# Batches 6 and 7 of an attention + ELU MLP kernel: their second layers as one product by seven half-size products, with attention ahead of the MLP

## The chip, the cores and the metric

The kernel runs on one core of a Trainium2 chip. The metric is the time of one execution on the device, in microseconds (us); lower is better. TensorE is called PE here (its weight loads PEld), VectorE DVE, ScalarE ACT, GpSimd POOL; SP issues the DMAs. Each engine works through its own instructions in the order in which the program issues them, and waits where an operand or a room is not ready.

## The reference

```python
def reference(q, k, v, g_q, g_k, w_in, w_out):   # q, k, v: 8 x 12 x 448 x 64
    q_n, k_n = rmsnorm(q, g_q), rmsnorm(k, g_k)  # over the last axis, eps 1e-6
    attn = softmax(q_n @ k_n.T / sqrt(64)) @ v   # for each batch and head
    x = attn.transpose(0, 2, 1, 3).reshape(8 * 448, 768)
    h = x @ w_in                                 # 768 x 2048
    g = where(h > 0, h, exp(min(h, 0)) - 1)
    return g @ w_out                             # 2048 x 768
```

## The kernel before

All products of the MLP are made with f16 operands, each f32 operand split in a high and a low f16 half; of the four partial products three are kept (high x high, high x low, low x high). So a first layer of a batch (`whi`, `wli` against `x`) is 16 rows `f` of 128 hidden units x 6 chunks x 3 = 288 matmuls of 448 columns, 18 to a row, and a second layer (`who`, `wlo` against `gts[f]`, the halves of g) is 6 rows `d` x 16 x 3 = 288. Products go to three PSUM banks in turn (`t_mo`); five more hold scores and the attention output.

Attention works in pairs of heads, six to a batch, a pair in seven tiles of 128 rows of scores: `s_burst` or `s_mm` (PE), `s_max` (DVE), `s_exp` (ACT), `s_z` (POOL), `s_rec` (DVE), `s_hi` (ACT), `s_lo` (DVE), a transposing DMA `s_tr`, then `attend` (PE) and `x_high`, `x_low`, which write the pair's chunk of x into one of nine rooms `xs`. Norms, halves and shifts of q, k and v are spread over POOL, DVE and ACT.

The order of all instructions is fixed by the program. Up to half step 264 (`H0`) it is a written list (`SCHED`); this part holds batches 0 and 1 of the MLP and is not touched. From there, two half steps make a tile of attention: in each half step `h` the tasks put at `h` are issued, and as many matmuls of the MLP as keep a steady rate (`RATE`, 6.86 in a half step). A product that ends at `h` puts its further steps at `h` plus the numbers in `SCHED` (`m1`, `m2`, `last1`, `last2`). After `LAST` (half step 700) seven matmuls are issued in each half step. `m1_out` is what follows a product of the first layer: `one` (ACT, exp), `two` (DVE), `three` (DVE, reads the product in PSUM and is its last reader), `four` (ACT, high half), `five` (DVE, low half).

The second layer of the last batch alone is already made by a scheme of seven products (Winograd's form of Strassen's): w_out is cut in 2 x 2 blocks (output rows `d` and `d + 3`, hidden rows `c` and `c + 8`), g in 2 x 2 blocks (hidden halves, and halves of 224 columns of the batch). Seven products of 24 matmuls of 224 columns for each of three `d` make it 504 matmuls of half width instead of 288 of full width. What the scheme needs of sums of weight blocks is made in twelve pieces beside attention (`piece_sums`, eight operations on DVE, two on ACT, two DMAs to DRAM, f32). At the end `t_steps` loads them back and splits them into halves (ACT and DVE, 24 operations each). The sums of the blocks of g are made in `m1_last` (ACT and DVE).

Of the kernel before, what the change touches and what calls it, by code (L numbers as in the profile page):

```python
# [33 lines left out]
def tile_attention_then_elu_mlp(ctx: ExitStack, tc: tile.TileContext, qk, v, v_scan, gg, w_in, w_out, out):  # L34
# [476 lines left out]
    def m_steps(b):  # L511
# [3 lines left out]
        sc = u = am = ui = ns = None  # L515
# [7 lines left out]
        def powers():  # L523
            nonlocal sc, u, am, ui, ns
# [6 lines left out]
            mscale[b] = sc, ui, u, ns, nui  # L531
# [8 lines left out]
        def inverse():  # L540
            ibits(ui, u, -1, ALU.mult, 254 * E, ALU.add)
            if b == 0:
                mul(mscale[b][4], ui, -1.0)
                mul(ns, ns, ui)

        def most_of():
# [5 lines left out]
            lambda: mul(u, am, vpow[b], 2.0 ** (-12 + UP)),  # L552
            inverse,
        ]
# [148 lines left out]

    def x_high(p):
        nc.scalar.activation(
            xs[p % NX][:, 0], av[:, :S], AF.Copy, scale=vscale[0] if by_pe(p * NJ) else 1.0
        )

    def x_low(p):
        x = xs[p % NX]  # L710
# [75 lines left out]
    HS, KF = S // 2, NF // 2  # L786
    scales = {}

    def joint_scales():

        t = pool.tile([128, 128], F32, tag="dgz", name="joint", bufs=2)
        pw, mx, rho1, rho2, uas_, aj, ui2 = (
# [3 lines left out]
        scales.update(rho1=rho1, rho2=rho2, uas=uas_, aj=aj, ui2=ui2)  # L796
# [7 lines left out]
    TS = ("t2", "t1", "t3", "t4")  # L804
    kept = [dram.tile([128, 4, 3, 256], F32, name=f"kept{d}") for d in range(3)]
    kept4 = [dram.tile([128, 4, 1, 256], F32, name=f"kept4{d}") for d in range(3)]
    tail = raws[:, 5 * S : 5 * S + 768].bitcast(F32)

    def piece_sums(d, r):

        A, Y, Z = (tail[:, a : a + 256] for a in range(0, 768, 256))
        W = None
        k = 4 * d + r
        rho = lambda i: scales[f"rho{i}"][:, k : k + 1]

        def full(o, row, kh):
            rows = slice(kh * KF, kh * KF + KF)
            h, l = (t[d + 3 * row][:, rows, 32 * r : 32 * r + 32] for t in (who, wlo))
            nc.vector.tensor_tensor(
                out=o.rearrange("p (f n) -> p f n", f=KF), in0=h, in1=l, op=ALU.add  # L820
            )

        def tt(o, x, y, op):
            nc.vector.tensor_tensor(out=o, in0=x, in1=y, op=op)

        def stt(o, x, i, y, op):
            nc.vector.scalar_tensor_tensor(
                out=o, in0=x, scalar=rho(i), in1=y, op0=ALU.mult, op1=op
            )

        def mul(o, i):
            nc.scalar.activation(o, o, AF.Copy, scale=rho(i))  # L832

        def fourth():
            nonlocal W
            W = pool.tile([128, 2 * S], F16, tag="p16", name="t4", bufs=3).bitcast(F32)[:, :256]
            full(W, 0, 1)
# [3 lines left out]
            lambda: mul(A, 1), lambda: tt(Z, Z, Y, ALU.subtract),  # L841
            lambda: stt(Y, Y, 2, A, ALU.subtract), lambda: mul(Z, 2), fourth,
            lambda: tt(A, Z, A, ALU.add),
            lambda: nc.sync.dma_start(
                out=kept[d][:, r], in_=tail.rearrange("p (q w) -> p q w", q=3)
            ),
            lambda: stt(W, W, 1, A, ALU.subtract),
            lambda: nc.sync.dma_start(out=kept4[d][:, r, 0], in_=W),
        ]

    stage = [t[:, a : a + 1024] for t, a in ((w32s, 0), (w32s, 1024), (wts, 0))]
    units = [
        t[:, a : a + 1024].rearrange("p (f r n) -> p f r n", f=KF, r=4)
        for t, n in (
            (raws.bitcast(F16), 6), (ptall.bitcast(F16), 6), (whis, 8), (wlis, 4),
        )
        for a in range(0, 1024 * n, 1024)
    ]
    part = [
# [37 lines left out]
    def t_step():  # L897
        if t_left:
            t_left.pop(0)()
# [774 lines left out]
UP = 13  # L1674
# [38 lines left out]
```

## Time and profile before

| | us |
|---|---|
| median of 3 runs | 1213.89 (1212.89 to 1215.51) |
| the profiled execution's own time | 1213.32 |
| its span, first to last instruction | 1211.2 |

The times are those of the program on the core. The rows further down come from the profiled execution; times in them count from the start of its span. `x24` is a number of instructions. "Busy" is the time in which at least one instruction of an engine was on record as running; a record that waits for something inside the chip counts as busy.

### The profile page before, as it was taken

The page shows a single profiled execution, that of the slowest core. Times are in us where ns is not written, and L with a number is a line of the kernel's source. Part 1 is how long each engine was busy: PE and PEld are TensorE (multiplying, and loading weights), DVE is VectorE, ACT ScalarE, POOL GpSimd, SP SyncE. Part 2 cuts the span into 40 slices and gives each one's busy share as a digit, 9 for nine tenths or more (in the row PEclk, how much of TensorE's full clock was granted, in tenths as well). Part 3 has the DMA queues.
Part 4 walks back from the last instruction along what each step waited for, and adds up shares of the span by engine and source line. Part 5 has one row for each costly group of instructions (what it writes and reads, how often), then busy time and mean ns, then how long its engine had stood idle before and what let it go on. Part 6 is the DMA issues. An engine that isn't in the chain of part 4 may idle for free. (4 is left out here: it accounts for less than half of the span.)

```text
span 1211.2 us, 22415 instructions
## 1 busy us (share of the span) xinstructions
PE 1168.8 (96%) x7396; PEld 632.7 (52%) x7396; DVE 1005.5 (83%) x2220; ACT 823.6 (68%) x1790; POOL 553.8 (46%) x799
## 2 busy tenths in 40 slices
PE   3789999999999999999999999999999999999998
PEld 2556555555455544445545545454554554555588
DVE  7999999888986699878997699878997799745962
ACT  6999999667866577656775577656776577644630
POOL 5887678654454343544444353544444454420000
PEclk9999999999999999999999999999999999999999
DMA  7876788868687866797669867797768976655200
GB/s 253 250 249 177 194 177 196 187 158 184 132 162 180 170 137 144 160 208 162 145 128 199 196 137 148 150 203 159 159 143 171 209 143 147 123 133 160 70 34 31
DMA packets 414531, 195.86 MB, mean 162 GB/s; under 512 B 369488, under 2 KB 394960, under 8 KB 414416
## 3 DMA queue, kind: packets, MB, share of 16 engines
q1 hardware_dynamic: 414416, 194.44, 70.8%
q8 instruction: 58, 0.95, 0.3%
q14 instruction: 57, 0.47, 0.1%
HBM read 74.65 MB, written 17.30 MB: 76 GB/s over the span
## 5 line engine op out<-in xcount | busy, mean ns | idle before, releaser
L625 POOL TENSOR_SCALAR st<-st 128x1 f32<-128x1 f32 x294 | 82.5, 281 | 400.5 <-ACT w32s L621 353.6
L605 DVE TENSOR_REDUCE st<-s 128x1 f32<-128x448 f32 x336 | 204.0, 615 | 52.8 <-PE s L598 42.2
L1134 PE MATMUL m<-gall,whos 128*128 128x448 f16 x896 | 242.7, 352 | 0.0
L621 ACT ACTIVATE w32s<-s,st 128x448 f32<-128x448 f32 x242 | 152.4, 630 | 104.6 <-DVE st L605 85.3
L1123 PE MATMUL m<-x,whis 128*128 128x448 f16 x816 | 221.0, 352 | 0.0
L671 DVE SCALAR_TENSOR_TENSOR raws<-w32s,st,raws 128x448 f16<-128x448 f32 x199 | 172.4, 867 | 30.8 <-ACT raws L665 30.4
L1134 PEld LDWEIGHTS <-whos 128*128 128x128 f16 x1344 | 130.7, 98 | 119.9 <-issue 1.8
L1123 PEld LDWEIGHTS <-whis 128*128 128x128 f16 x1344 | 130.3, 98 | 119.2 <-issue 2.7
L1134 PE MATMUL m<-gall,wlos 128*128 128x448 f16 x448 | 158.1, 353 | 0.0
L665 ACT ACTIVATE raws<-w32s,st 128x448 f16<-128x448 f32 x199 | 131.1, 663 | 22.1 <-DVE st L633 6.2
L1123 PE MATMUL m<-x,wlis 128*128 128x448 f16 x408 | 144.0, 353 | 0.0
L1134 PE MATMUL s<-gall,whos 128*128 128x448 f16 x448 | 121.3, 352 | 0.0
L598 PE MATMUL s<-qkt 128*64 128x448 f16 (+1 forms) x496 | 108.7, 363 | 12.8 <-DMA qkt<-t 4.9
L1123 PE MATMUL s<-x,whis 128*128 128x448 f16 x400 | 108.3, 352 | 0.2 <-DVE e L747 0.2
L1123 PEld LDWEIGHTS <-wlis 128*128 128x128 f16 x672 | 65.7, 98 | 69.7 <-issue 11.1
L1134 PEld LDWEIGHTS <-wlos 128*128 128x128 f16 x672 | 65.7, 98 | 69.3 <-issue 10.6
L407 POOL TENSOR_TENSOR nat<-nat,r 128x896 f32<-128x896 f32 (+1 forms) x48 | 87.3, 1819 | 31.7 <-DVE r L397 23.8
L698 PE MATMUL av<-ptall,vt 128*64 128x448 f16 x924 | 95.1, 353 | 0.0
L752 ACT ACTIVATE gall<-e,ui 128x448 f16<-128x448 f32 x96 | 63.8, 667 | 39.5 <-DVE e L747 39.4
L1134 PE MATMUL s<-gall,wlos 128*128 128x448 f16 x224 | 79.0, 353 | 0.0
L758 DVE SCALAR_TENSOR_TENSOR gall<-e,ui,gall 128x448 f16<-128x448 f32 x96 | 74.3, 775 | 1.3 <-ACT gall L752 1.3
L698 PEld LDWEIGHTS <-vt 128*64 128x64 f16 x924 | 52.0, 110 | 36.9 <-issue 3.2
(256 smaller groups left out, 2333.5 us busy)
## 6 DMA issues: line engine op xcount, KB each, us to landing
nat<-in_qk SPq DMA_DIRECT2D x48, 448.0 KB, 4.5
raws<-in_w_out SPq DMA_DIRECT2D x24, 512.0 KB, 4.2
qkt<-qkt SPq DMA_DIRECT2D x96, 112.0 KB, 4.1
out<-y SPq DMA_DIRECT2D x47, 224.0 KB, 2.4
vn<-in_v SPq DMA_DIRECT2D x38, 256.0 KB, 3.1
vscan<-in_v_scan SPq DMA_DIRECT2D x36, 224.0 KB, 3.3
whos<-in_w_in SPq DMA_DIRECT2D x10, 768.0 KB, 7.6
raws<-in_w_in SPq DMA_DIRECT2D x6, 768.0 KB, 7.2
```

The lines of the kernel that those rows point to most:

```text
L407: nc.gpsimd.tensor_tensor(out=n[:, a:], in0=n[:, a:], in1=r[:, a:], op=ALU.mult)
L598: nc.tensor.matmul(ps[r0 : r0 + n, :S], lhs, qq[:, 1, h * S : h * S + S], start=(t == 0), stop=(t == 2),)
L605: nc.vector.tensor_reduce(out=st[:, 0:1], in_=pss[T][:, :S], axis=AX.X, op=ALU.max, negate=True)
L621: nc.scalar.activation(e, ps, AF.Exp, bias=st[:, 0:1], accum_out=st[:, 1:2])
L625: (nc.vector if by_pe(T) else nc.gpsimd).tensor_scalar(out=st[:, 1:2], in0=st[:, 1:2], scalar1=1e-9, scalar2=2.0 ** (UP - 7) if by_pe(T) e ...
L665: nc.scalar.activation(p16[:, :S], e, AF.Copy, scale=stats[T][:, 2:3])
L671: nc.vector.scalar_tensor_tensor(out=p16[:, S:], in0=e, scalar=r, in1=p16[:, :S], op0=ALU.mult, op1=ALU.subtract)
L698: nc.tensor.matmul(av[64 * h : 64 * h + 64, :S], vs[:, h], ps[h], start=(k == 0), stop=(k == len(terms) - 1),)
L752: nc.scalar.activation(g[:, 0], e, AF.Copy, scale=1.0 if b == 0 else ui)
L758: nc.vector.scalar_tensor_tensor(out=g[:, 1], in0=e, scalar=ui, in1=g[:, 0], op0=ALU.mult, op1=ALU.subtract)
L1123: nc.tensor.matmul(ph[:, :S], w[:, c, :], x[:, r, :], start=(c == 0 and i == 0), stop=last)
L1134: nc.tensor.matmul(py[:, :S], w, g[:, r, :], start=(f == 0 and i == 0), stop=last)
```

## The change

The second layers of batches 6 and 7 become one product by seven. The two column halves are now the two batches of 448 columns. Batch 6 has its first layer as the other batches have it; then six products (`mid`) give the output rows `d` of batch 6 and with them `c11`, the first of the seven; then comes the first layer of batch 7, and then the other fifteen products (five for each of three `d`), all 448 columns wide: 6 x 24 + 15 x 24 = 504 matmuls.

- Both batches share one scale: `powers` takes the larger of the two `vpow`, `m_two` puts that earlier.
- `piece_sums` now writes high and low f16 halves to DRAM, four DMAs to a piece, by way of one room (`staging`, gained by putting both `k_up` into one room). Of its operations four (`full`) stay on DVE, twelve are on POOL, four copies on ACT. `SCHED["sums"]` puts a step of it every 1.18 half steps, before one every 2.7.
- The loads and splits of `t_steps` are replaced by 24 loads (`t_load`) straight into the rooms of `whis` and `wlis`, as the rows of the first layer of batch 7 are used up.
- `m1_last` is new: after `one`, `two` and `third` (as `three` before) it needs the difference of the two batches' g in place of batch 6's, and three more sums. `full` (POOL) adds batch 6's halves back to f32; the further steps are on DVE (`stt`, one `low_of`), ACT (`high`) and POOL (`full`, two sums, two `low_of`).
- Attention has three more rooms for x, and the rate of the MLP is set so that the first layer of batch 7 begins at half step 682 (`AHEAD`): from half step 264 on (3888 - 1179) / 418 = 6.48 matmuls in a half step.

```diff
-    k_up = [t.bitcast(F16)[:, :S] for t in rooms[NE : NE + 2]]
+    k_up = [rooms[NE].bitcast(F16)[:, a : a + S] for a in (0, S)]
     p_rooms = [t.bitcast(F16) for t in rooms[NE + 2 : NE + 2 + NP16]]
+    staging = rooms[NE + 1].bitcast(F16)[:, :512].rearrange("p (i n) -> p i n", i=2)
...
+            vp = vpow[b]
+            if b == B - 2:
+                vp = small("vp", bufs=1)
+                nc.vector.tensor_tensor(out=vp, in0=vpow[b], in1=vpow[b + 1], op=ALU.max)
...
-            mscale[b] = sc, ui, u, ns, nui
+            mscale[b] = (sc, *mscale[b - 1][1:]) if b == B - 1 else (sc, ui, u, ns, nui)
...
+    places, x_of = list(xs), {}
+
     def x_high(p):
+        if p == 3 * NPAIR:
+            for _ in range(3):
+                t = pool.tile([128, 2 * S], F16, tag="p16", name="xe", bufs=3)
+                places.append(t.rearrange("p (i s) -> p i s", i=2))
+        x_of[p] = places.pop(0)
...
+            o = o.rearrange("p (f r n) -> p f r n", f=2, r=4)
+            r = scales[f"rho{i}"][:, 4 * d : 4 * d + 4]
+            tt(o, o, r.unsqueeze(1).unsqueeze(3).broadcast_to([128, 2, 4, 32]), ALU.mult)
+
+        def split(o, q):
...
+            lambda: mul(A, 1), lambda: tt(Z, Z, Y, ALU.subtract), lambda: mul(Y, 2),
+            lambda: tt(Y, Y, A, ALU.subtract), lambda: mul(Z, 2),
+            *split(Y, "t1"),
+            lambda: tt(A, Z, A, ALU.add), lambda: full(Y, 0, 1),
+            *split(Z, "t3"),
+            lambda: mul(Y, 1), lambda: tt(Y, Y, A, ALU.subtract),
+            *split(A, "t2"), lambda: None, lambda: None,
+            *split(Y, "t4"),
...
+    def t_load(d, q):
+        for i in (0, 1):
+            nc.sync.dma_start(
+                out=part[d, q][i].rearrange("p c n -> p (c n)"), in_=kept[d][q][:, i]
+            )
...
+    def mid(d, kh, bank):
+        def first():
+            c11[d] = as_f32(places.pop(0))
+            nc.scalar.activation(c11[d], bank[:, :S], AF.Copy, scale=uas[d][0])
+
+        def second():
+            y = pool.tile([128, S], F32, tag="e", name="y", bufs=3)
+            more(y, bank, c11[d], uas[d][0])
+            return y
+
+        if kh == 0:
+            return "mid0", 0, [first]
+        y = []
+        return "mid1", 0, [lambda: y.append(second()), lambda: store(y[0], d, B - 2)]
...
+        c = f % KF
+        low = f < KF
+        g = gts[f]
+        e1, e2, r1, r2, r3, r4 = temps[c % 2]
+        e = e1 if low else e2
...
+        def third():
+            nc.vector.scalar_tensor_tensor(
+                out=e, in0=ph[:, :S], scalar=sc, in1=e, op0=ALU.mult, op1=ALU.max
+            )
+
+        def full(o):
+            nc.gpsimd.tensor_tensor(out=o, in0=g[:, 0], in1=g[:, 1], op=ALU.add)
+
+        def stt(o, x, s1, y, op):
+            nc.vector.scalar_tensor_tensor(out=o, in0=x, scalar=s1, in1=y, op0=ALU.mult, op1=op)
+
+        def high(o, x, s1=1.0):
+            nc.scalar.activation(o[:, 0], x, AF.Copy, scale=s1)
+
+        def low_of(eng, o, x):
+            eng.tensor_tensor(out=o[:, 1], in0=x, in1=o[:, 0], op=ALU.subtract)
+
+        if low:
+            return "last1", 0, [
+                one, two, third, lambda: full(r1),
+                lambda: stt(r2, e, scales["nui2"], r1, ALU.add),
+                lambda: high(g, r2), lambda: low_of(nc.gpsimd, g, r2),
+            ]
+        o1, o2, o3 = three
+        return "last2", 0, [
+            one, two, third, lambda: full(r4),
+            lambda: high(g, e, ui2),
+            lambda: nc.gpsimd.tensor_tensor(out=r3, in0=e1, in1=e2, op=ALU.add),
+            lambda: stt(g[:, 1], e, ui2, g[:, 0], ALU.subtract),
+            lambda: high(o1, r3, ui2), lambda: stt(r1, r3, ui2, r1, ALU.subtract),
+            lambda: high(o2, r1),
+            lambda: nc.gpsimd.tensor_tensor(out=r4, in0=r4, in1=r1, op=ALU.subtract),
+            lambda: stt(o1[:, 1], r3, ui2, o1[:, 0], ALU.subtract),
+            lambda: high(o3, r4), lambda: low_of(nc.vector, o2, r1),
+            lambda: low_of(nc.gpsimd, o3, r4),
+        ]
+
...
+    def mlp_two():
+        yield from first_layer(B - 2, range(NF), lambda k, f, ph: m1_out(B - 2, f, ph))
+        for d in range(3):
+            for kh in (0, 1):
+                bank = t_mo()
+                fs = range(kh * KF, kh * KF + KF)
+                for last in product(
+                    bank, lambda c: (who[d][:, fs[c]], wlo[d][:, fs[c]]), lambda c: gts[fs[c]]
+                ):
+                    yield mid(d, kh, bank) if last else None
+        t_left.extend((-(-4 * (i + 1) // 3) - 1, dq) for i, dq in enumerate(T_ORDER))
+        yield from first_layer(
+            B - 1, [k // 2 + k % 2 * KF for k in range(NF)], m1_last
+        )
+        for h in range(h_now[0] + 1, h_now[0] + 12):
             now, tasks[h] = tasks.get(h, []), []
             for fn, args in now:
...
+        for d, q in (
+            (0, "t3"), (0, "t4"), (1, "t3"), (1, "t4"), (0, "t1"), (0, "t2"), (0, "c22"),
+            (1, "t1"), (1, "t2"), (1, "c22"), (2, "t3"), (2, "t4"), (2, "t1"), (2, "t2"),
+            (2, "c22"),
+        ):
+            bank = made[d, q] = banks[n % 8]
+            n += 1
+            for _ in product(bank, lambda c: w_of(d, q, c), lambda c: b_of(q, c)):
+                yield None
+            ub, uj = uas[d][1:]
+            if q == "t2":
+                u2, u3, u4 = (as_f32(places.pop(0)) for _ in range(3)) if d < 2 else ys[0]
+                ys[d] = u2, u3, u4
+                more(u2, bank, c11[d], uj)
+                more(u4, made[d, "t1"], u2, uj)
+                more(u3, made[d, "t3"], u2, uj)
+                for k, row in (("t4", d), ("t1", d + 3)):
+                    y = pool.tile([128, S], F32, tag="e", name="y", bufs=3)
+                    more(y, made[d, k], u3, uj)
+                    store(y, row, B - 1)
+            if q == "c22":
+                y = pool.tile([128, S], F32, tag="e", name="y", bufs=3)
+                more(y, bank, ys[d][2], ub)
+                store(y, d + 3, B - 2)
...
-    START = HB + X_LAG
     LAST = 2 * NCHUNK + 28
+    pace = None
...
-        want = int((h + 1 - START) * RATE)
+        if pace is None:
+            base, pace = done, (FIRST_LAYER - done) / (AHEAD - h)
+        want = base + int((h + 1 - H0) * pace)
...
-    "scales": 671,
-    "sums": [272, 2.7],
-    "parts": [[676, 0.6], [690, 1.2], [716, 0.8]],
-    "last1": [[1, 2, 3, 4, 4, 5, 5, 6]],
-    "last2": [[1, 2, 3, 4, 4, 5, 5, 6]],
+    "scales": 640,
+    "m_two": [600, 602, 603, 604, 606],
+    "sums": [272, 1.18],
+    "mid0": [[1]],
+    "mid1": [[1, 2]],
+    "last1": [[1, 2, 3, 2, 4, 5, 6]],
+    "last2": [[1, 2, 3, 2, 4, 4, 5, 5, 6, 7, 7, 7, 8, 8, 9]],
...
-MLP_STEPS = 2 * 3 * (B - 1) * NF * NC_ + 3 * NF * NC_ + 3 * 7 * 12 + 1
+MLP_STEPS = 2 * 3 * (B - 2) * NF * NC_ + 2 * 3 * NF * NC_ + 3 * 7 * 24 + 1
+FIRST_LAYER, AHEAD = 2 * 3 * (B - 2) * NF * NC_ + 3 * NF * NC_ + 3 * 2 * 24, 682
 UP = 13
-RATE = 576 / (2 * PB)
-X_LAG = 8
```

## Rows read from the trace of the kernel before

**Rows 1.** Windows by stage: busy us (instructions) by engine, granted clock, DMA share, GB/s

```profile
60.00:90.00 30.00, 25.35 (x233) 17.18 (x233) 29.62 (x70) 27.46 (x59) 24.52 (x22) 1.00 0.77 248
133.40:200.10 66.70, 65.17 (x434) 34.45 (x430) 63.19 (x144) 62.62 (x131) 49.33 (x64) 1.00 0.83 186
969.00:1037.80 68.80, 68.80 (x406) 34.58 (x405) 65.65 (x138) 52.98 (x114) 32.47 (x46) 1.00 0.68 140
1105.10:1159.40 54.30, 54.30 (x289) 28.09 (x288) 47.75 (x100) 34.24 (x60) 0.00 (x0) 1.00 0.30 92
1159.50:1207.80 48.30, 48.30 (x506) 48.21 (x503) 18.25 (x38) 6.22 (x12) 0.00 (x0) 1.00 0.07 26
```

The columns of busy time are PE, PEld, DVE, ACT and POOL. The stages are a first layer in the written list (batch 0), the first layer of batch 6, the first layer of batch 7, and its second layer.

**Rows 2.** Chain that ended last, batch 7: start us, us, engine, product, line, matmuls

```profile
1105.23 3.40 PE m L1021 x18
...
1129.07 3.40 PE s L1021 x18
...
1187.31 4.60 PE m L1058 x48
1191.91 16.11 PE s L1058 x168
```

**Rows 3.** Timeline of DVE, the last `more`: start us, us

```profile
1208.05 0.45 DVE L1066 SCALAR_TENSOR_TENSOR y<-s,joint,uu 128x224 f32<-128x224 f32 x1 [1.85 <-PE s L1058]
```

**Rows 4.** Single source lines on DVE: ns min/median/max, first and last start, form

```profile
L819 DVE TENSOR_TENSOR raws<-whos,wlos x36: 405/415/985, 434.7 to 1030.8; 128x256 f32<-128x256 f16 x36
...
L671 DVE SCALAR_TENSOR_TENSOR raws<-w32s,st,raws x199: 658/683/1933, 323.1 to 1093.0; 128x448 f16<-128x448 f32 x199
...
L736 DVE TENSOR_SCALAR e<-e x96: 369/383/1221, 284.8 to 1039.7; 128x448 f32<-128x448 f32 x96
...
L747 DVE SCALAR_TENSOR_TENSOR e<-m,sc,e x64: 659/672/685, 285.4 to 1043.0; 128x448 f32<-128x448 f32 x64
...
L421 DVE TENSOR_TENSOR nat<-nat,gst x42: 599/616/1504, 9.8 to 1043.7; 128x448 f32<-128x448 f32 x42
```

These are `full` of the sums, `s_lo`, `two`, `three` and `q_gain`.

**Rows 5.** DMA issues: KB each, median us from issue to landing

```profile
out<-y SPq DMA_DIRECT2D x47, 224.0 KB, 2.4
...
wts<-kept SPq DMA_DIRECT2D x4, 512.0 KB, 5.2
...
kept<-t SPq DMA_DIRECT2D x12, 128.0 KB, 2.1
...
out<-y SPq DMA_DIRECT2D x2, 112.0 KB, 1.8
```

**Rows 6.** Single source lines on POOL, columns as in rows 4

```profile
L756 POOL TENSOR_TENSOR gall<-e,gall x16: 1033/1037/1602, 144.4 to 212.5; 128x448 f16<-128x448 f32 x16
...
L421 POOL TENSOR_TENSOR nat<-nat,gst x6: 1134/1482/1834, 21.7 to 105.1; 128x448 f32<-128x448 f32 x6
...
L472 POOL TENSOR_TENSOR vt<-vn,vt x38: 1154/1157/1542, 226.9 to 1085.4; 128x512 f16<-128x512 f32 x38
...
L407 POOL TENSOR_TENSOR nat<-nat,r x48: 1180/1690/2327, 8.6 to 1032.9; 128x896 f32<-128x896 f32 x47, 128x448 f32<-128x448 f32 x1
```

**Rows 7.** Timelines of DVE and POOL at two places

```profile
702.01 1.45 DVE L671 SCALAR_TENSOR_TENSOR raws<-w32s,st,raws 128x448 f16<-128x448 f32 x1
703.38 0.61 DVE L605 TENSOR_REDUCE st<-s 128x1 f32<-128x448 f32 x1
...
701.76 1.21 POOL L430 TENSOR_TENSOR t<-nat,t 128x448 f16<-128x448 f32 x1
...
709.89 0.41 DVE L819 TENSOR_TENSOR raws<-whos,wlos 128x256 f32<-128x256 f16 x1
...
710.82 1.50 DVE L671 SCALAR_TENSOR_TENSOR raws<-w32s,st,raws 128x448 f16<-128x448 f32 x1
...
709.83 2.01 POOL L407 TENSOR_TENSOR nat<-nat,r 128x896 f32<-128x896 f32 x1
```

**Rows 8.** Timeline of DVE, the third step behind the eighth product of batch 7

```profile
1134.35 0.68 DVE L937 SCALAR_TENSOR_TENSOR x<-s,sc,x 128x448 f32<-128x448 f32 x1
```

More of the change, by code (lines that the diff above doesn't have):

```diff
@@ L551, in m_steps @@
             scales,
-            lambda: mul(u, am, vpow[b], 2.0 ** (-12 + UP)),
+            lambda: mul(u, am, vp, 2.0 ** (-12 + UP)),
             inverse,
-        ]
+        ] if b < B - 1 else [powers, lambda: None, scales, lambda: None, lambda: None]
     def cuts(j):
@@ L826, in stt @@
[L826 to L829, printed above, removed]
-        def mul(o, i):
[L832 to L837, printed above, removed]
+            rows = slice(kh * KF + 2 * k, kh * KF + 2 * k + 2)
+            h, l = (t[d + 3 * row][:, rows].rearrange("p f n -> p (f n)") for t in (who, wlo))
@@ new lines, in m1_last, with one, two @@
+    def m1_last(k, f, ph):
+        sc, ui2 = (t[:, a : a + 1] for t, a in ((mscale[B - 1][0], f), (mscale[B - 1][1], 0)))
+        if not spots:
+            spaces()
+        c = f % KF
[3 more added lines that the diff above has]
+        e = e1 if low else e2
+        three = [as_f16(spots[i]) for i in range(3 * c, 3 * c + 3)]
+        sums.update(zip([("t1", c), ("t2", c), ("c22", c)], three))
+        def one():
+            nc.scalar.activation(e, ph[:, :S], AF.Exp, scale=sc)
+        def two():
+            nc.vector.tensor_scalar(
+                out=e, in0=e, scalar1=-1.0, scalar2=0.0, op0=ALU.add, op1=ALU.min
+            )
+        def third():
+            nc.vector.scalar_tensor_tensor(
+                out=e, in0=ph[:, :S], scalar=sc, in1=e, op0=ALU.mult, op1=ALU.max
[13 more added lines that the diff above has]
+                lambda: high(g, r2), lambda: low_of(nc.gpsimd, g, r2),
+            ]
+        o1, o2, o3 = three
[10 more added lines that the diff above has]
+            lambda: low_of(nc.gpsimd, o3, r4),
+        ]
@@ L1023, in mlp_last, with product @@
                     )
-                    yield m1_last(k, f, ph) if last else None
-        for h in range(h_now[0] + 1, h_now[0] + 8):
+                    if last and f == order[-1]:
+                        places.extend(x_of.pop(b * NPAIR + c) for c in range(NC_))
+                    yield result(k, f, ph) if last else None
+            while t_left and t_left[0][0] <= k:
+                t_load(*t_left.pop(0)[1])
+    def product(bank, w, x):
+        for c in range(KF):
+            for i, (a, r) in enumerate(((0, 0), (0, 1), (1, 0))):
+                nc.tensor.matmul(
+                    bank[:, :S], w(c)[a], x(c)[:, r],
+                    start=c == 0 and i == 0, stop=c == KF - 1 and i == 2,
+                )
+                yield c == KF - 1 and i == 2
@@ L1125, in mlp @@
                     )
+                    if last and f == NF - 1:
+                        places.extend(x_of.pop(b * NPAIR + k) for k in range(NC_))
                     yield m1_out(b, f, ph) if last else None
```

306 lines of the change are left out of this document (79 added, 227 removed).

## Prediction

> **What bounds the kernel now.** The page's first part counts PE as busy nearly throughout; a busy PE need not be a fast one, so next come the windows by stage: from 133 us on PE is busy for whole stages (68.80 of 68.80 us, 54.30 of 54.30, 48.30 of 48.30) at a granted clock of 1.00, which is the 2.4 GHz level [rows 1]. Third the chain that ended last: in the last batch seven products of 18 matmuls of 448 columns take 1129.07 - 1105.23 = 23.84 us, 189.2 ns each, and 48 of 224 columns take 1191.91 - 1187.31 = 4.60 us, 95.8 ns each [rows 2]. So the stage that changes is a queue of matmuls without gaps: a matmul less is time less, as long as nobody else makes PE wait. Who could? In a first layer beside attention DVE is busy 65.65 of 68.80 us and POOL 32.47; in the last first layer DVE 47.75 of 54.30 and POOL nothing [rows 1]. DVE has little to spare, POOL much.
>
> **The products.** Before, the second layer of batch 6 is 288 matmuls of 448 columns and that of batch 7 504 of 224: 288 x 0.1892 + 504 x 0.0958 = 54.5 + 48.3 = 102.8 us. After, both are 504 of 448 columns: 95.4 us. That is **-7.4 us** of PE time and all the change can win.
>
> **The end.** The last `more` is 448 instead of 224 columns wide: 0.67, as `three`, instead of 0.45 us [rows 3, 4]. The last store has 224 KB instead of 112: 2.4 instead of 1.8 us [rows 5]. With the longer last matmul **+0.9 us**.
>
> **Attention denser against the MLP, and the sums of weights.** The step rate falls from 6.86 to (3888 - 1179) / 418 = 6.48 matmuls per half step, so a first layer has 22.2 instead of 21 tiles beside it: DVE, ACT and POOL work of attention per PE time rises by 5 to 6%. Of the twelve pieces of sums DVE keeps four of eight operations, about 0.42 us each [rows 4], so it saves 12 x 4 x 0.42 = 20 us over the stage, which pays for that. ACT gets four copies for two products, about 1 us in a piece; it has room. POOL gets 12 x 12 = 144 operations of 256 columns. None is in the trace; at 448 columns one takes 1.04 us, at 512 1.16 [rows 6], 1.9 ns per column, so about 0.67 us, between 0.59 (in proportion to 448) and 1.04: 96 us of POOL, 17% of some 570 us. In a first layer POOL comes to 32.5 x 1.06 + 12 = 46 of 69 us. The SP queue gets 48 writes and 24 loads for 24 and 12; a load waits for the products of a few `f`, is of 256 KB (512 KB took 5.2 us [rows 5]) and is wanted some 40 us later. The staging room is refilled three steps, some 5 us, after its write is issued; a write of 128 KB took 2.1 us [rows 5], so I cost it at nothing; if SP is late, ACT waits there, and `s_exp` behind it. The nearest stage to all this is the window from 133 us: POOL 49.33 and DVE 63.19 of 66.7 us, PE 65.17 [rows 1], 1.5 us lost. Five such first layers (batches 2 to 6) bound it between 0 and 7.5 us; I take **+2.5**, a third, since DVE was fuller there. `s_rec` on DVE waits for `s_z` behind POOL's new work; that is in it.
>
> **The first layer of batch 7: the dear step.** PE makes two products (a pair, `f` = `c` and `c + 8`) in 36 x 0.1892 = 6.81 us. Per pair the new `m1_last` issues:
> on POOL six operations of 448 columns: two `low_of`, which have just the form of a row (1.04), two `full` (f16 to f32, not in the trace, 1.04 to 1.13) and two of f32 (1.13 [rows 6]), **6.4 us**. POOL alone is then 94% full.
> On DVE two `two` at 0.38, two `third` at 0.67, and five with both inputs in SBUF at 0.62 to 0.68 [rows 4]: 5.5 us. On ACT seven, at the 34.24 us for 60 of this stage before [rows 1] 4.0 us, which fits.
> Alone either engine fits. But the trace shows that such operations don't run at the same time. At 701.76 POOL begins an operation of the form that takes 1.04 alone, at 702.01 DVE one of 0.68; they take 1.21 and 1.45, and both are done at 703.46, 1.70 us for 1.72 us of work. At 709.83 a POOL operation of 1.69 alone meets two on DVE of 0.42 and 0.68: 2.49 us for 2.79 [rows 4, 6, 7]. `two` is hit as well (0.38 in the median, 1.22 at the most); `third`, which reads PSUM, is not (at most 0.69 in 96) [rows 4].
> So per pair: POOL 6.4, DVE's five and two `two` 4.1, less 0.5 because a DVE record overlaps the one before by 0.08 (703.38 against 703.46 [rows 7]): 10.0 us, and less the tenth that the second collision saved: **9.0 us for a pair** against PE's 6.81. In bounds: 6.81 if it all fits, 10.5 if nothing overlaps. I take 9.0, as the second collision has DVE and POOL work in about the mixture of this stage.
>
> The Trainium skill (GPSIMD Engine Reference, Specifications and Engine selection) speaks against this change twice: it says that GpSimd shares its SBUF interface with VectorE, which contend when DVE has two SBUF inputs or a two-port mode, and that two-input elementwise work takes about twice as long on GpSimd and belongs on VectorE. By the first the collisions above are the rule, and the trace agrees. By the second, six times 2 x 0.62 would be 7.4 us of POOL for a pair, an estimate, and the sum below would come to some 1227 us; the rows have 1.13 against 0.62 for one operation that both engines run [rows 4, 6].
>
> Why PE feels it: `third` frees the bank of its product, PE has three, so PE starts product k + 3 only when `third` of k is done, a slack of 6.81 us after product k ends. `third` stands in DVE's queue behind `g1`, `r1`, `o1`, `o2` of the pair before; `r2` and `r1` wait for POOL's `full` and `r3`, and POOL's `full` of two pairs on waits for DVE's `o2`: neither can run ahead. With the layer starting at 0, product 2 ends at 10.2; its `third` ends at about 13 (before, product 7 ended at 1129.07 + 3.40 = 1132.47 and its `third` at 1135.03 [rows 2, 8]). From there 9.0 a pair: `third` of product 12 at 13 + 45 = 58, so product 15 starts at 58 instead of 51.2, **6.8 us** late. Then (0, t3) wants `g` of row 7: `third` of product 14 ends at 67, then `r2` behind one POOL operation, ACT's copy, POOL's `low_of`, 3.6 us: 70.6. PE gets there at 58 + 3.4 + 21 x 0.19 = 65.4 and waits **5.2 us**. The three products after it, 13.7 us, cover the rest of the sums. Together **+12.0**; in general 6 x pair - 42, so 0 at 7.0 or less, 21 at 10.5. PE would be busy 55 of 62 us there; at 25.35 of 30 us the clock was 1.00 [rows 1], so no price for the clock.
>
> **Sum.** Against the profiled execution's own 1213.3 us: -7.4 + 0.9 + 2.5 + 12.0 = +8.0, **1221.3 us**. The median of the runs before is 1213.9, 0.6 higher, within their scatter.
>
> **Rivals.**
> A, faster: the collisions stay behind PE. A pair needs 7.0 us or less: POOL's `full` of f16 much shorter than 1.04, or POOL's queue filling the times in which DVE reads PSUM or waits for ACT. For it: PE hid a DVE at 95% and a POOL at 74% for 66 us. Against it: those busy times hold the collisions already, and here POOL's work alone is 94%. Time: -7.4 + 0.9 + 1 = -5.5, 1207.8. It decides from a pair of 7.6 us, where stall and saving cancel.
> B, the sums hurt too: POOL's 96 us collide with `s_lo` and `g1` in first layers that are 95% full on DVE, `s_rec` and so `s_exp` come late, PE waits for banks of scores. Price the upper bound and a little, 10 instead of 2.5: 1228.8. Against it: the stage from 133 us.
> C, no change: a pair of 7.3 to 8.0 us, stall 2 to 6, within 2.4 us of before.
>
> **How the numbers follow.** Forecast 0.48, A 0.26, B 0.14, C 0.12. 0.2% is 2.4 us, about what a measurement of this kernel can tell from nothing. Slower by more: forecast and B, 0.62; within: C, 0.12; faster: A, 0.26. The range leaves out the outer edges of A and B: 1207 to 1230; the forecast's own, with a pair of 8.3 to 9.8 us, is 1217 to 1227.
>
> **What would show it.** In the profile after: 504 matmuls of 448 columns at 189 ns in the last two second layers; in the first layer of batch 7 POOL over 90% busy, its operations and DVE's two-input ones well above 1.04 and 0.68; PE idle before products, released by DVE's `third`, some 7 us; one wait of some 5 us in (0, t3), released by POOL. Before that stage PE gaps of a few us in all. Wrong: POOL and DVE records overlapping without growing, the layer in 55 us, or gaps above 8 us before it.

## The result and the profile after

The changed kernel takes 1229.95 us (median of 4 runs, 1229.27 to 1233.49) against 1213.47 for the kernel before: a ratio of 1.0139 with a 95% interval of 1.0116 to 1.0162, so slower by 16 us where 8 were forecast. Its profiled execution took 1229.63 us, its span 1227.8.

The windows by stage of the changed kernel, columns as in [rows 1]: the whole stretch from batch 2's first layer to batch 7's, three pieces of it (a second layer and the first layer after it, and the last first layer beside attention), then the first layer of batch 7, and the fifteen products.

```profile
411.60:1088.20 676.60, 666.11 (x3904) 333.43 (x3902) 583.43 (x1180) 458.13 (x1028) 413.41 (x609) 1.00 0.78 160
482.80:554.10 71.30, 69.64 (x409) 34.92 (x408) 58.71 (x119) 45.22 (x106) 48.03 (x72) 1.00 0.92 185
554.10:627.30 73.20, 70.85 (x411) 34.87 (x410) 69.94 (x133) 53.61 (x122) 47.98 (x69) 1.00 0.70 146
985.00:1055.00 70.00, 70.00 (x411) 34.78 (x409) 63.22 (x136) 51.30 (x114) 34.77 (x56) 1.00 0.70 135
1088.20:1149.30 61.10, 56.40 (x288) 28.53 (x287) 52.95 (x59) 27.14 (x46) 46.53 (x36) 0.97 0.30 99
1149.50:1224.00 74.50, 69.88 (x361) 35.55 (x359) 24.67 (x32) 6.08 (x10) 13.51 (x11) 0.98 0.08 29
```

The same stretch and one first layer in it, of the kernel before:

```profile
412.40:1105.10 692.70, 690.54 (x4047) 346.31 (x4046) 576.08 (x1232) 458.94 (x1010) 298.11 (x469) 1.00 0.75 160
554.60:623.30 68.70, 68.70 (x405) 34.49 (x404) 65.60 (x138) 53.08 (x114) 32.25 (x46) 1.00 0.69 146
```

Read stage by stage. The long stretch, called the attention stage from here on, has 144 matmuls of 448 columns fewer, 27.2 us at 0.1892; before it would have been 692.7 - 27.2 = 665.5, now it is 676.6: **+11.1 us**. The last stage should be 54.3 us [rows 1] and 360 x 0.1892 = 68.1; it is 61.1 and 74.5: **+13.2 us**. The products save their 7.4 us. That is +16.9 for a span that grew by 16.6.

What PE waited for, the attention stage (releaser; us in total, times, longest us):

```profile
PE s L587 <- ACT w32s L626: 5.9, 9, 1.7
PE m L1103 <- DVE e L759: 2.4, 3, 1.2
PE av L703 <- issue: 1.2, 1, 1.2
```

and the last stage:

```profile
PE m L1015 <- DVE x L972: 3.7, 2, 2.1
PE s L1027 <- POOL gall L986: 2.5, 1, 2.5
PE s L1027 <- ACT gall L983: 2.1, 1, 2.1
PE s L1015 <- DVE rt L972: 1.0, 1, 1.0
```

In the first list PE waits for a bank of scores that an exponential (`s_exp`, L626) still has to read, and for a bank of the MLP that `three` (L759) has to free; `L1103` is a first layer. In the second stand the waits that were forecast: `third` (L972) frees the banks late, and the first product wants `g` of the last rows. Their sum is 9.3 of 13.2 us. In most of the rest PE worked at a lower granted clock. PE's timeline and the windows there:

```profile
1134.21 0.55 PE L1015 MATMUL m<-x,whis 128*128 128x448 f16 x2 [2.14 <-DVE x L972]
1134.58 0.55 PE L1015 MATMUL m<-x,wlis 128*128 128x448 f16 x1
```

```profile
1134.80:1137.80 3.00, 3.00 (x9) 1.21 (x8) 2.85 (x4) 1.77 (x4) 2.44 (x3) 0.50 0.01 4
1138.60:1142.00 3.40, 3.40 (x20) 1.76 (x19) 3.40 (x4) 1.20 (x2) 3.40 (x4) 1.00 0.12 30
1158.80:1161.80 3.00, 3.00 (x9) 1.21 (x8) 2.20 (x4) 1.34 (x2) 2.23 (x2) 0.50 0.03 5
```

Behind a wait of 2.1 us, and again behind 2.1 and 2.5, PE makes 9 matmuls in 3.0 us, 0.33 us each, at a granted clock of 0.50 (the 1.2 GHz level), and then 20 in 3.4 us at 1.00. Only the second fall cost time. The first stood, but for 0.2 us, in the place of a wait: it came in product 12, counted from 0, and product 14 began at 1142.70, 0.2 us after the end of the `third` that frees its bank (that of product 11, 1141.82 + 0.67), so at the full clock PE would have had to wait there. The timeline of `third` for products 2, 11 and 12, and PE's start of product 14:

```profile
1100.63 0.67 DVE L972 SCALAR_TENSOR_TENSOR rm<-m,sc,rm 128x448 f32<-128x448 f32 x1
...
1141.82 0.67 DVE L972 SCALAR_TENSOR_TENSOR rt<-m,sc,rt 128x448 f32<-128x448 f32 x1
...
1144.43 0.67 DVE L972 SCALAR_TENSOR_TENSOR x<-m,sc,x 128x448 f32<-128x448 f32 x1
```

```profile
1142.70 0.54 PE L1015 MATMUL m<-x,whis 128*128 128x448 f16 x2
```

The new instructions on POOL: three kinds of the sums (`mul`, f32 and low half), and three of the last first layer (`full`, `low_of`, `r3`):

```profile
L832 POOL TENSOR_TENSOR raws<-raws,joint x48: 607/614/1014, 434.1 to 1004.7; 128x256 f32<-128x256 f32 x48
L832 POOL TENSOR_TENSOR raws<-raws x48: 725/733/1130, 439.4 to 1006.9; 128x256 f32<-128x256 f32 x48
L832 POOL TENSOR_TENSOR wts<-raws,wts x48: 664/686/1182, 449.7 to 1018.1; 128x256 f16<-128x256 f32 x48
...
L977 POOL TENSOR_TENSOR rm<-gall x4: 1032/1416/1421, 1073.4 to 1147.4; 128x448 f32<-128x448 f16 x4
...
L986 POOL TENSOR_TENSOR gall<-rn,gall x4: 1037/1180/1409, 1096.4 to 1148.8; 128x448 f16<-128x448 f32 x4
...
L998 POOL TENSOR_TENSOR rn<-x,x x4: 1134/1244/1276, 1097.3 to 1151.3; 128x448 f32<-128x448 f32 x4
```

Alone (the shortest of each) they take about what was estimated (0.61 to 0.73 for 0.67, 1.04 and 1.13), and in the last first layer they stand stretched, as do DVE's in these rows (`two`, 0.38 alone [rows 4], and the low half of `g`):

```profile
L967 DVE TENSOR_SCALAR rt<-rt x4: 1217/1220/1319, 1105.1 to 1156.5; 128x448 f32<-128x448 f32 x4
...
L980 DVE SCALAR_TENSOR_TENSOR gall<-x,ui,gall x4: 979/1215/1226, 1097.8 to 1151.9; 128x448 f16<-128x448 f32 x4
```

### The profile page after: what moved, and what is told of

Read it like the earlier page. It is cut to its first block, busy times and chain, and to the rows that moved or that the text cites. A ratio compares the mean times of both kernels' runs of the same rounds, so it can differ in the third digit from the quotient of the medians.

```text
span 1227.8 us, 22061 instructions
## 1 busy us (share of the span) xinstructions
PE 1168.1 (95%) x7108; PEld 608.5 (50%) x7108; DVE 1024.3 (83%) x2122; ACT 815.0 (66%) x1792; POOL 729.0 (59%) x985
## 5 line engine op out<-in xcount | busy, mean ns | idle before, releaser
L626 ACT ACTIVATE w32s<-s,st 128x448 f32<-128x448 f32 x242 | 152.1, 629 | 121.9 <-DVE st L610 103.9
L610 DVE TENSOR_REDUCE st<-s 128x1 f32<-128x448 f32 x336 | 203.5, 613 | 30.9 <-PE s L603 22.2
L1116 PE MATMUL m<-gall,whos 128*128 128x448 f16 x768 | 209.7, 353 | 0.0
L1103 PEld LDWEIGHTS <-whis 128*128 128x128 f16 x1152 | 111.2, 98 | 110.8 <-issue 11.4
L1116 PEld LDWEIGHTS <-whos 128*128 128x128 f16 x1152 | 111.0, 98 | 107.9 <-issue 8.3
L1103 PE MATMUL m<-x,whis 128*128 128x448 f16 x578 | 157.6, 353 | 2.4 <-DVE e L759 2.4
L1116 PE MATMUL m<-gall,wlos 128*128 128x448 f16 x384 | 135.4, 353 | 0.0
L1116 PE MATMUL s<-gall,whos 128*128 128x448 f16 x384 | 105.3, 353 | 0.4 <-DVE gall L770 0.4
L1103 PE MATMUL m<-x,wlis 128*128 128x448 f16 x289 | 101.9, 353 | 0.0
L1103 PEld LDWEIGHTS <-wlis 128*128 128x128 f16 x576 | 56.3, 98 | 54.2 <-issue 3.3
L1103 PE MATMUL s<-x,whis 128*128 128x448 f16 x286 | 77.8, 352 | 0.3 <-DVE e L759 0.2
L1116 PE MATMUL s<-gall,wlos 128*128 128x448 f16 x192 | 67.7, 353 | 0.0
```

The costliest lines, as they stand in the source:

```text
L610: nc.vector.tensor_reduce(out=st[:, 0:1], in_=pss[T][:, :S], axis=AX.X, op=ALU.max, negate=True)
L626: nc.scalar.activation(e, ps, AF.Exp, bias=st[:, 0:1], accum_out=st[:, 1:2])
L1103: nc.tensor.matmul(ph[:, :S], w[:, c, :], x[:, r, :], start=(c == 0 and i == 0), stop=last)
L1116: nc.tensor.matmul(py[:, :S], w, g[:, r, :], start=(f == 0 and i == 0), stop=last)
```

## The experiments

All medians stand beside 1212.7 to 1213.8 us for the kernel before on the same chip. Theories: **collisions** (POOL's and DVE's instructions with two SBUF inputs run in turn, which fills the last first layer and stretches the others), against **density** (tiles of attention closer together make DVE the bound of the first layers, whatever POOL does) and **queue** (other work on POOL waits behind the sums). Stage times come from one execution of each version. For the versions in which the sums are taken apart it lies 1.1 to 1.8 us under the median of the runs, for the changed kernel 0.3, so differences between their stages are good to some 2 us.

### The sums, taken apart

`sums_idle` leaves out all arithmetic of the sums of weights (their rooms hold zeros); the DMAs stay.

```
...
     def full(o, row, kh):
...
-            nc.vector.tensor_tensor(out=o, in0=h, in1=l, op=ALU.add)
+            pass
     def tt(o, x, y, op):
+            return
             nc.gpsimd.tensor_tensor(out=o, in0=x, in1=y, op=op)
...
-                lambda: nc.scalar.activation(staging[:, 0], o, AF.Copy),
+                lambda: None,
...
```

> All arithmetic of the sums of weights is left out (DVE, ACT and POOL; the 48 writes and 24 loads stay and carry zeros), so the seven products of the last two batches are wrong. Theory sums (POOL's 144 operations collide with DVE beside attention): PE's gaps between the first layer of batch 2 and that of batch 7 fall from some 13 us to 4 or less, 1219 to 1222 us. Theory density (fewer MLP matmuls to a tile of attention make DVE the bound): the gaps stay, 1228 to 1231 us.

`sums_no_pool` leaves out POOL's twelve instructions of a piece only (the `return` alone).

> Only POOL's twelve operations of each piece of sums are left out (DVE's four, ACT's four copies and the DMAs stay; the sums are wrong). Theory sums by POOL's collisions: as without any arithmetic, 1219 to 1222 us, and s_lo on DVE falls from 903 ns back to about 870. If instead the staging room, ACT's copies or the DMAs were the cause: 1227 us or more.

`sums_memset` puts three memsets of a room that is not in use in the place of each.

```
...
-            nc.gpsimd.tensor_tensor(out=o, in0=x, in1=y, op=op)
+            for _ in range(3):
+                nc.gpsimd.memset(rooms[NE + 1][:, 256:448], 0.0)
```

> The changed kernel, with each of the 144 POOL instructions of the sums of weights replaced by three POOL memsets of a 128x192 f32 piece of a room that nothing uses then. POOL stays occupied at the same places, but reads no SBUF operands; the low halves of the sums' products are zeros and the combinations are not formed (the six DVE additions of a piece, the ACT copies and the DMAs stay). Without POOL's instructions the attention stage (batch 2's first layer to batch 7's) had taken 666.6 us, with them 676.6. Theory collisions (POOL's two-input instructions stretch DVE's two-input instructions, which bound the dense first layers): the stage goes back to 666 to 669, the run to about 1221. Theory queue (the per-tile scalar of the softmax waits on POOL behind the sums): the stage stays at 674 to 677, the run at about 1230.

Measured: 1217.54 us (1.0031, 1.0016 to 1.0046), 1221.19 (1.0071, 1.0056 to 1.0086) and 1227.52 (1.012, 1.0105 to 1.0135). The attention stage of the three, in this order:

```profile
411.90:1074.20 662.30, 662.09 (x3902) 332.28 (x3901) 535.83 (x1133) 443.58 (x980) 294.11 (x465) 1.00 0.79 164
```

```profile
411.60:1078.20 666.60, 663.57 (x3903) 332.70 (x3902) 558.53 (x1181) 457.15 (x1028) 293.54 (x465) 1.00 0.80 163
```

```profile
410.80:1083.50 672.70, 664.94 (x3903) 332.94 (x3902) 563.75 (x1181) 458.63 (x1028) 403.69 (x897) 1.00 0.79 161
```

Without the sums the denser attention costs nothing: 662.3, PE busy throughout. The DVE additions and ACT copies add 4.3 us (3.7 by the medians). Holding POOL for 110 us without reading operands adds 6.1 (6.3), in which DVE's busy time grows by 5.2. The real instructions, which read operands and hold POOL for 120 us, add the last 3.9 (676.6; by the medians 2.4), and with them DVE's busy time goes from 563.8 to 583.4 us: that is the stretch. So holding POOL costs at least as much as the stretch does.

In what the copies add there is a wait that the prediction had put at nothing: ACT stood 6.2 us in `sums_no_pool`, and 5.2 in the changed kernel, because the room `staging` had not yet been written out (`t<-wts` is the write; the line is of the changed kernel). No copy of ACT waited for POOL there.

```profile
ACT wts L841 <- DMA t<-wts: 5.2, 5, 2.1
```

`before_dense` gives the kernel before the changed kernel's pace (6.48 instead of 6.86 matmuls per half step, with the rooms for that) and leaves its sums and products as they were.

```
...
-        want = int((h + 1 - START) * RATE)
+        if pace is None:
+            base, pace = done, (FIRST_LAYER - done) / (AHEAD - h)
+        want = base + int((h + 1 - H0) * pace)
...
-RATE = 576 / (2 * PB)
...
+FIRST_LAYER, AHEAD = 3888, 682
```

> The kernel before with nothing of the change but the pace of 6.48 matmuls in a half step and three more rooms for x; the last 156 matmuls of batch 6 are made behind attention. Matmuls are as many as before. Theory density: some 9 us slower than before, 1222. Theory sums: within 3 us of before, 1211 to 1217.

Measured: 1220.06 us (1.0063, 1.0047 to 1.0079); its stage:

```profile
412.90:1110.90 698.00, 692.95 (x4048) 347.42 (x4046) 577.00 (x1232) 456.43 (x1010) 297.62 (x469) 1.00 0.76 158
```

698.0 - 27.2 = 670.8 against 665.5 at the old pace: density costs 5.3 us with before's sums, and the new form of the sums the other 5.8 of 11.1. Density costs nothing where DVE and POOL have no sums (`sums_idle`), so it is the two together that cost; the new form of the sums at the old pace was not run. The sums on POOL were meant to pay for the density; they cost as much again.

### The last first layer

`last_no_pool` leaves out POOL's six instructions of a pair (DVE and ACT read other operands, so the combinations are wrong).

```
-            nc.gpsimd.tensor_tensor(out=o, in0=g[:, 0], in1=g[:, 1], op=ALU.add)
+            pass
...
-            lambda: nc.gpsimd.tensor_tensor(out=r3, in0=e1, in1=e2, op=ALU.add),
...
+            lambda: None,
...
```

> POOL's six operations for each pair of products in the first layer of batch 7 are left out (DVE and ACT keep theirs, on other operands; results of the last two batches are wrong). By the collisions of this stage: the layer takes 54.5 us instead of 61.1, the wait in the first of the fifteen products and both falls of the clock go, 1216 to 1219 us. If DVE alone were too slow there: 1226 us or more.

`last_on_dve` computes everything: five of the six go to DVE (the expectation says six; the low half of `o3` stayed on POOL), and `two` goes to ACT as a Relu with signs turned.

```
...
-            nc.vector.tensor_scalar(
-                out=e, in0=e, scalar1=-1.0, scalar2=0.0, op0=ALU.add, op1=ALU.min
-            )
+            nc.scalar.activation(e, e, AF.Relu, scale=-1.0, bias=1.0)
...
-                out=e, in0=ph[:, :S], scalar=sc, in1=e, op0=ALU.mult, op1=ALU.max
+                out=e, in0=ph[:, :S], scalar=nsc, in1=e, op0=ALU.mult, op1=ALU.min
...
-            nc.gpsimd.tensor_tensor(out=o, in0=g[:, 0], in1=g[:, 1], op=ALU.add)
+            nc.vector.tensor_tensor(out=o, in0=g[:, 0], in1=g[:, 1], op=ALU.add)
...
```

> The changed kernel, with batch 7's first layer moved off POOL: the six POOL instructions of a pair of blocks go to DVE, and in exchange DVE's instruction on exp minus one goes to ACT as a Relu, with the sign carried by the constants; everything is computed. Theory collisions: a pair costs DVE 13 instructions at their unstretched 0.55 to 0.65 us, 7.2 to 7.6 us, against PE's 6.81 and against some 9 us now: the last first layer falls from 61.1 to 55 to 58 us, the wait in the first product shrinks to under 3 us, the granted clock keeps its upper level and the run is 1217 to 1221. Theory that DVE's amount of work alone is the limit: 13 instead of 8 instructions make a pair no shorter, the layer stays at 61 or above and the run at 1230 or above.

Measured: 1218.05 us (1.0045, 1.003 to 1.006) and 1218.08 (1.0046, 1.0029 to 1.0063). Layer and products of `last_on_dve`:

```profile
1088.80:1143.10 54.30, 54.30 (x289) 28.09 (x288) 48.45 (x83) 34.26 (x63) 12.92 (x6) 1.00 0.32 111
1143.30:1212.00 68.70, 68.13 (x361) 35.10 (x359) 20.24 (x33) 5.33 (x10) 3.35 (x2) 1.00 0.09 32
```

DVE issues 83 instructions in this layer instead of 59, having taken over five of POOL's six and given up only `two`, and is busy for less time, 48.45 instead of 52.95 us; the layer is at its 54.3. That shows the collisions, and 12.6 of the 13.2 us come back. `full` on DVE, its mean in ns behind the busy time (on POOL it took at least 1032, in the L977 line above):

```profile
L979 DVE TENSOR_TENSOR rm<-gall 128x448 f32<-128x448 f16 x4 | 2.5, 614 | 0.0
```

The granted clock stays at 1.00: without PE's waits it didn't fall.

### What POOL's sums delay

Three attempts to get at the queue, on the changed kernel: `s_z`, the 128x1 instruction between exponential and reciprocal, on DVE (`z_on_dve`) or on ACT (`z_on_act`), and the sums handed out in second layers only (`sums_in_second`).

```
-        (nc.vector if by_pe(T) else nc.gpsimd).tensor_scalar(
+        (nc.vector if by_pe(T) or T >= 132 else nc.gpsimd).tensor_scalar(
```

> The changed kernel, with the 128x1 instruction between the exponential and the reciprocal (s_z) on VectorE instead of POOL for all tiles from batch 2 on; everything is computed. Theory queue: reciprocals no longer wait behind POOL's sums, the stage falls from 676.6 to 667 to 670 us and the run to about 1222. Theory collisions: DVE, which is the bound of the first layers, gets some 200 more short instructions of 0.1 to 0.15 us while its stretch by POOL stays: the stage stays or grows to 680 to 690, the run is 1230 to 1240.

```
         nc.scalar.activation(e, ps, AF.Exp, bias=st[:, 0:1], accum_out=st[:, 1:2])
+        if not by_pe(T):
+            nc.scalar.activation(st[:, 1:2], st[:, 1:2], AF.Copy, scale=2.0**-7)
...
```

> The changed kernel, with the 128x1 instruction between exponential and reciprocal (s_z) on ScalarE, right behind the exponential, instead of on POOL; the added 1e-9 is left out, as the sum is at least 1. Everything else is computed. In the stage from batch 2's first layer to batch 7's, POOL's sums had cost 10.0 us, of which 6.1 remained when POOL was held as long by memsets. Theory queue (the reciprocal waits for s_z behind POOL's sums, and DVE's queue stands behind the reciprocal): those 6 go, the stage takes 669 to 672 us instead of 676.6 and the run 1222 to 1225 us. Theory that POOL's sums delay other work of POOL (V's parts, the normalising of Q and K) or that collisions on DVE are all of it: the stage stays at 675 to 678, the run at 1229 to 1231. ACT gets 294 instructions of about 0.2 us, some 40 us over the stage, of which it has 458 busy of 677.

```
...
-    "sums": [272, 1.18],
+    "sums": [0, [(306, 349), (395, 438), (484, 527), (573, 616), (661, 680)]],
```

> The changed kernel, with the steps of the sums of weights handed out only in the half steps in which the MLP is in second-layer products, where it puts no activation on DVE; everything is computed. Theory collisions with DVE as the bound of the first layers: the stage falls from 676.6 to 665 to 670 us (as without POOL's instructions or a little less), the run to 1219 to 1224. Theory that the density alone sets it, or that POOL's place doesn't matter: the stage stays at 674 to 677 and the run at 1228 to 1231. Loss if the sums are now packed too densely for POOL: above 1231.

Measured: 1241.58 us (1.0238, 1.0222 to 1.0255), 1253.06 (1.0319, 1.0299 to 1.034) and 1239.58 (1.0218, 1.0201 to 1.0235), all worse than the change. PE's two waits in the stage of `sums_in_second`, and a wait of ACT there:

```profile
PE av L703 <- DMA ptall<-raws: 9.4, 7, 4.2
PE s L587 <- ACT w32s L626: 8.4, 6, 2.1
```

```profile
ACT wts L841 <- DMA t<-wts: 46.4, 24, 3.9
```

The attention products wait for transposes of the probabilities (`ptall<-raws`), and for exponentials, that come late. But this run changed two things: packed into second layers, the sums stand almost twice as close together (312 steps in 191 half steps, before in 367), and ACT, which makes the exponentials and the high halves, stood 46.4 us for the room `staging` (5.2 in the changed kernel). So it doesn't show whether the tiles in second layers have room for POOL's hold.

With `s_z` on ACT, DVE's largest wait in the stage is the first line here; the second is the same wait in the changed kernel:

```profile
DVE raws L679 <- ACT raws L673: 44.3, 61, 2.6
```

```profile
DVE raws L676 <- ACT raws L670: 22.8, 39, 1.8
```

So neither engine takes 0.14 to 0.2 us more on each tile's way from the exponential to its low half without loss. That `s_z` itself waits behind the sums is little of it. Three waits for POOL in the stage, of DVE for `s_z` (in the changed kernel and in `sums_memset`) and of ACT for `ua`, the factor with which a second layer's output is scaled (changed kernel):

```profile
DVE st L638 <- POOL st L630: 1.2, 3, 0.8
```

```profile
DVE st L638 <- POOL st L630: 2.5, 4, 1.1
```

```profile
ACT y L791 <- POOL ua L783: 6.2, 5, 2.6
```

The wait for `ua` is 6.5 us in `sums_memset`, and there is none in the kernel before or in `sums_no_pool`. It is the largest that the sums add on POOL, and behind it stand ACT's exponentials; that PE's stops come from it is not shown.

`last_on_dve_z_on_act`, that edit and `last_on_dve` in one, took 1239.17 us where 1211 to 1214 or 1218 was expected. `sparser_sums`, the same with the sums 1.33 half steps apart, took 1237.6, where 1210 to 1212, 1 to 2 us less than the other, or no change was expected. Both missed their level by more than 20 us, and their intervals overlap. On the kernel before:

> The kernel before, with s_z on ScalarE alone. POOL had no sums there, s_rec waited 5.5 us for POOL in all, and in the stage PE was stopped for 0.7 us. Queue theory: there was hardly a queue, so 1212 to 1214 us, no change. If a shorter way from the exponential to the reciprocal is worth something in itself: under 1211.

1216.22 us (1.0027, 1.0017 to 1.0037): a loss there too.

### Giving DVE room

On top of `last_on_dve`, two ways to relieve DVE in first layers: an uneven pace (fewer tiles beside first layers, more beside second ones), or every `two` on ACT as in the diff above.

```
...
-        want = base + int((h + 1 - H0) * pace)
...
+        left = 1.0
+        while left > 0:
+            end = (int(reach + 1e-6) // 288 + 1) * 288
+            r = pace[int(reach + 1e-6) % 576 // 288]
+            dt = min(left, (end - reach) / r)
+            reach, left = reach + dt * r, left - dt - 1e-9
+        want = int(reach + 1e-6)
```

> As last_on_dve (1218 us; stage from batch 2's first layer to batch 7's 677.1 us), with the pace of the MLP uneven: 6.86 matmuls per half step in first layers, as before, and 6.11 in second layers, the same 6.48 on average and the same end of attention. Everything is computed. Theory (DVE is the bound of the dense first layers, where it is busy 67 to 70 of 70 to 73.5 us, and has 10 us of room in the second): first layers lose their stalls of 1.4 to 4.7 us each, the stage falls to 666 to 671 us and the run to 1207 to 1212. Rival (the amount of work on POOL and in the loop of DVE and ACT sets it, wherever the tiles stand; or second layers then stall as they did with the sums packed into them): the stage stays at 674 to 680, the run at 1215 to 1221.

> The same with 7.20 in first and some 5.85 in second layers. Theory: first layers now free of stalls, second layers at 1.11 times the density of the average; if these have room, as uneven_686 or 1 to 2 us better; if their transposes come late, as in sums_in_second, worse than uneven_686 by 3 or more. Rival: no change from last_on_dve.

> As last_on_dve, with the exp-minus-one instruction of every batch's first layer (two, 0.38 us on DVE) on ACT as a Relu (some 0.56 us), sign carried by the constants; even pace. DVE is relieved of 16 x 0.38 = 6 us in a first layer, ACT gets 9 on top of 53 of 73. Theory (DVE is the bound): the stage falls to 668 to 672 us, the run to 1209 to 1213. Rival (the loop through ACT is as full, as with s_z on ACT, where DVE waited 20 us more for ACT's high parts): the stage grows to 680 or more, the run to 1221 or more.

Measured: 1221.38 us (1.0063, 1.0047 to 1.0079), 1218.19 (1.0047, 1.0032 to 1.0063) and 1211.09 (0.998, 0.997 to 0.9989). With the uneven pace the stage took 678.2 and 677.0 us; its first layers from batch 3 on were faster (69.8, 68.7, 69.2 and 68.8 us at 6.86), and PE waited for late transposes instead:

```profile
PE av L703 <- DMA ptall<-raws: 4.5, 3, 2.1
PE s L587 <- ACT w32s L626: 3.2, 5, 1.4
```

So moving tiles moves the stall. Taking work from DVE removes it: in `two_on_act` the stage fell to 663.8 us, but an interruption in batch 1's first layer let batch 2 start at 419.0 instead of 411.6. (Both together, `uneven_two_on_act`, took 1216.81, between the two, where 1205 to 1211 was expected.) The last pair leaves batches 0 and 1 alone, on `last_on_dve` and on the kernel before:

```
...
         def two():
...
+            if b > 1:
+                nc.scalar.activation(e, e, AF.Relu, scale=-1.0, bias=1.0)
+                return
...
```

> As two_on_act (1211 us), but from batch 2 on only. Batch 1's first layer, which had a stall of 8.6 us in two_on_act, is as in the changed kernel. Theory (DVE is the bound of the dense first layers): the stage takes 663 to 666 us as in two_on_act, and the run 1202 to 1206 us, 0.6 to 0.9 per cent under before. Rival (the late start of batch 2 in two_on_act is what gave its stage room): the stage grows back to 668 to 672 and the run is 1208 to 1212.

> The kernel before with the same edit, from batch 2 on. Theory: in the kernel before DVE was full but not late (PE was stopped for 2.1 us between 412 and 1105 us), so at most 2 us can be won: 1211 to 1213 us. Rival (a gain of its own): 1208 or less. With a loss through ACT: above 1214.

Measured: **1206.52 us (0.9935, 0.9922 to 0.9948)**, 0.5 above the range expected, and 1209.39 (0.9961, 0.9948 to 0.9974). The stage of `two_from_batch_2`, a first layer in it, and its last two stages; then the stage of `before_two_on_act`:

```profile
412.30:1077.40 665.10, 663.07 (x3903) 332.34 (x3902) 554.55 (x1109) 492.67 (x1108) 407.48 (x607) 1.00 0.80 163
...
554.50:624.90 70.40, 70.09 (x410) 34.81 (x409) 66.20 (x119) 60.56 (x136) 46.23 (x69) 1.00 0.74 156
1077.40:1131.70 54.30, 54.30 (x289) 28.09 (x288) 48.49 (x83) 34.31 (x63) 12.94 (x6) 1.00 0.32 111
1131.90:1200.60 68.70, 68.11 (x361) 35.07 (x359) 20.21 (x33) 5.30 (x10) 3.35 (x2) 1.00 0.09 32
```

```profile
411.70:1101.50 689.80, 689.21 (x4047) 346.17 (x4046) 546.71 (x1161) 490.41 (x1090) 293.29 (x469) 1.00 0.76 161
```

With DVE's busy time down from 583.4 to 554.6 us the stage is 665.1, 11.5 shorter, although POOL is held as before (407 us) and ACT has 35 us more. That is 2.8 us above `sums_idle`, with all the sums in place. So POOL's hold is cheap where DVE has room: its 6.1 us are a price beside a full DVE, not one that adds to whatever else is done. This version beats the kernel before and the changed one. The kernel before gains 4.4 us by the edit, more than the 2 expected; what the change itself is worth with both repairs is 1209.4 - 1206.5 = 2.9 us of its 7.4: the stage gives back 665.1 - (689.8 - 27.2) = 2.5, the products 0.6, and the rest of the kernel the remainder. The intervals of the two versions just touch.

## Why the prediction was right and wrong

- **The products:** right. 504 matmuls of 448 columns in place of 288 and 504 narrow ones; without waits the 360 of the last stage take 67.9 us in `last_no_pool`, 0.1886 each, where the sum had 0.1892.
- **The first layer of batch 7:** right in mechanism, place and size. +12.0 was forecast, +13.2 measured. From product 2 to product 12 `third` came 1144.43 - 1100.63 = 43.8 us later, 8.8 us for a pair where 9.0 was worked out; the layer ended at 61.1 where 54.3 + 6.8 = 61.1 was worked out, and the wait in the first product was 2.1 + 2.5 us for 5.2. The runs without POOL's instructions show that it was POOL. "No price for the clock" was wrong by some 1.9 us: the second fall to 0.50, 3.4 us long, cost half of that, and the first some 0.2, as PE would have waited for `third` in its place. One sign didn't come: POOL was busy 46.5 of 61.1 us in that layer, 76% and not over 90, while DVE was the fuller engine (52.95).
- **"Attention denser against the MLP, and the sums of weights":** the step that failed. +2.5 was taken out of 0 to 7.5; it was +11.1, above its own upper bound. The mechanism that was named is part of it: 10.0 of the 14.3 us that the sums cost at this pace are POOL's, and POOL's instructions do collide with DVE's in full first layers. That reciprocals wait behind POOL is hardly seen (DVE's waits for `s_z` are 1.2 us in the stage). The size failed on three assumptions. First, "it saves 20 us ..., which pays for that": DVE's four operations left DVE, but POOL's stretched its others by 20 us, so DVE's busy time rose from 576.1 to 583.4 us in a shorter stage, and the 5.3 us that density costs were not paid for. Second, the stage from 133 us was used as a bound; there POOL's long instructions stand beside a DVE that is 95% busy for a single layer, with 19 tiles of attention beside it (19 `s_max` in that window) instead of the 22.2 of the new pace, and without the sums. Third, the staging room was costed at nothing: ACT stood 5.2 us for it; what of this reaches PE was not separated. Rival B named the failure with 10 us in the place of 2.5 and gave 1228.8, the nearest to what was measured.
- **The end:** +0.9 was forecast; the time from the last matmul to the end of the span grew by some 0.3 us, from 3.2 to 3.5.
- **The two rules of the Trainium skill** (GPSIMD Engine Reference, Specifications and Engine selection): the first, that GpSimd and VectorE contend when VectorE reads two SBUF operands, is what `last_on_dve` and `sums_memset` show, with 24 DVE instructions more in 4.5 us less. The second, about twice the time for two-input work on GpSimd, is somewhat high here: the shortest `full` took 1.03 us on POOL and 0.61 on DVE, 1.7 times.
- **Left open:** through which of POOL's waiting instructions the 6.1 us of the hold act. `s_z` is not the main one by DVE's waits, 2.5 us in `sums_memset`; `ua` is the largest wait seen, 6.5 us there. DVE's busy time also grew by 5.2 us under the memsets, so not all of the 6.1 need be a queue.

## What to carry to other kernels

Moving work to an engine with idle time helps only if it doesn't use what the full engine uses: here 144 POOL instructions of 0.6 to 0.7 us stretched DVE by 20 us, about what they were to take from it. Look for the engine that is full in one stage, and ask of each instruction on it who waits for its result: `two` moved from DVE to ACT gave 11.5 us back, `s_z` moved from POOL to ACT, with the same ACT time in all, cost 18.5. That the second stands on each tile's way from exponential to low half, and the first doesn't, is our reading of the two. And before a change spends a stage's slack (here by a pace 6% denser), price what already lives on it.

## What had not been expected of the hardware

After PE had stood for 2.1 us, following an earlier stop of 1.6, in a stage in which it was otherwise busy, the granted clock was 0.50 for about 3.4 us; that happened twice (the second time after 2.1 and 2.5 us), and not in the three versions whose waits in that stage were 0.6 us or less (`last_no_pool`, `last_on_dve`, `two_from_batch_2`). And POOL memsets of 128x192 took 0.26 us each and left DVE's busy time almost as it was (563.8 against 558.5), while about as much POOL time in two-input instructions (120 us for 110) added 20 us more: what stretches DVE is mostly that POOL reads operands, not that POOL is busy.
